# Linear attention with a mixture block on one Trainium2 core: a written-out order of operations in place of planner ranks, and one transfer for w_phi

## The chip, the cores and the metric

The kernel runs on one core of a Trainium2 chip. The metric is the device time of one execution in microseconds, measured on the chip; runs of the same kernel are given with their median, lowest and highest. The inputs are float32 and lie in DRAM, as does the output. The engines are named as in the profile: PE (TensorE, the matrix engine, with PEld for its weight loads), DVE (VectorE), ACT (ScalarE), POOL (GpSimd) and SP (SyncE, which here only issues transfers).

## The reference

Two blocks follow each other. The first is a linear attention with a feature map `phi`, over 8 batches, 8 heads, 576 positions and 64 features per head; the second normalises the rows, applies two dense layers with a ReLU between them and adds the residual.

```
phi(x):  proj = x @ w_phi                      # 64 -> 128 features
         proj = proj - max(abs(proj), axis=-1)
         return concat(exp(proj), exp(-proj))  # 256 features
q_p, k_p = phi(q), phi(k)
kv  = einsum('bhsf,bhsd->bhfd', k_p, v);  z = sum(k_p over s)
out = (q_p @ kv) / (q_p @ z + 1e-6)            # per batch and head
x   = out, heads side by side                  # 8 x 576 x 512
xn  = (x - mean) / sqrt(var + 1e-6) * g_ln
y   = x + relu(xn @ w_ch1) @ w_ch2             # 512 -> 2048 -> 512
```

## The kernel before, in words

**Units.** The attention is done in 32 units, each with two heads. Of the 576 positions 512 are the main part (four chunks of 128 rows per head) and 64 the tail; the tails of the two heads lie side by side in one chunk of 128. A unit loads q, k and v (L676), brings q and k to bfloat16 with the features on the partitions, projects them with w_phi on PE (`pm` for the main part, L984 and L990; `px` for the tails, L943 and L944; `pt` for the transposed projection of q, L999), takes the largest magnitude per row on DVE (L1047 main, L947 tails), takes the exponentials on ACT (L1067, L1111), multiplies v by the scale of k on POOL (L1074 to L1080), sums k against v on PE (L1135, L1141, in `n_bank`), casts the sum (`KV`, L1149 on DVE or L1151 on ACT), multiplies q's features by it (`num`, L1199, L1205), collects and inverts the denominator on DVE (L1221, L1227, L1233) and writes the quotient on POOL as rows of x (L1266, L1270; L1166 moves tails by a transfer). Units 0 to 7 are transposed on PE (L829, L837, copied out of PSUM at L844 on DVE or L846 on ACT); from unit 8 on the inputs are cast (L902 and its neighbours) and transposed by DMA, issued on SP (L921).

**The dense block.** Rows of x are taken in nine groups of 512 tokens. The statistics are taken on DVE (L1338, L1350), the rows are centred and scaled (L1355 on DVE, L1360 on ACT, L1364 on POOL), transposed on PE (L1302) and copied (L1312 on DVE, L1314 on ACT). Then come the first layer (L1431, ReLU at L1439 on DVE or L1441 on ACT) and the second (L1463, with the residual at L1471 to L1480). The last groups go another way (L1597, and L1780 for a product with fewer multiplications). The weights are loaded on POOL's queue: w_ch1 in two pieces at L769, w_ch2 in two at L787.

**What sets the order.** Nothing of the main work is issued where it is written. Each piece is given to the class `Order` (L327) with `add`: the engines that could do it, an estimated time on each, the keys that it reads and writes, the PSUM banks that it takes and gives back, and a rank. `run` then goes through an estimated timeline, event by event: whenever an engine is free there, it takes the ready operation of the lowest rank. The rank is the latest start that the estimates allow, plus an offset from a table, `OFF`, of 32 dictionaries with an entry for each stage. Where several engines could do an operation, the first that is free takes it. The list that comes out is what is issued, engine by engine, and on the chip every engine goes through its own list strictly in order, each instruction waiting for what it needs.

**Fillers.** Up to 75 us of the estimated timeline (`WARM`), whenever PE has nothing ready there, `run` puts a matmul of zeros on PE (`fill`, L2063 and L2064; the first, L2061, stands ahead of it). These matmuls are in the program, so they run whether PE would have had to wait at that place or not.

**The beginning.** Before the planned work DVE clears tiles (L585 to L609), and two casts bring w_phi to the bfloat16 tile `wbk` (L612): rows 0 to 63 for the first head, rows 64 to 127 for the second. The tile `wphi_f` has w_phi twice, one copy per half of the partitions, by two transfers, one on ACT's queue (L564) and one on POOL's (L565). Behind the casts come more clears (`ea`, L616, and `vx`, L596 to L598). These stand in the code as they are issued; the planner only knows that DVE is busy with them.

## Time and profile before

| what | value |
|---|---|
| runs of the kernel | 357.18, 357.02, 356.86 us |
| median | 357.02 us |
| span of the profiled execution | 354.4 us, 9372 instructions |
| profiled execution's own time | the span and what lies around it; the runs' median is 2.6 us above the span |
| PE, DVE, ACT, POOL busy | 98%, 86%, 73%, 53% |
| granted clock of PE | 1.00 in the stretches read |

The profile shows one execution. A group's row has the busy time, the mean duration of one instruction in ns, and the idle time of the engine ahead of such instructions with what ended most of it. A timeline's row has the start in us from the beginning of the span, the time from the first start to the last end, engine, line, operation, tiles and the number of instructions taken together; in brackets stands the idle time ahead and what ended it. A table of stretches has the busy time of each engine between two times. PE's instructions overlap, so a group's mean duration is longer than the distance from one start to the next. Some matmul records are missing from a trace.

### The profile page before, as it was taken

To read this page: it belongs to the slowest core of one execution; us is meant where nothing else is said; L and a number is where in the kernel's file an instruction comes from. 1 tells how busy PE (TensorE), PEld (TensorE's weight loads), DVE (VectorE), ACT (ScalarE), POOL (GpSimd) and SP (SyncE) were. 2 spreads that over 40 slices of the span, in tenths; PEclk is the share of its full clock that TensorE was granted. 3 is DMA by queue.
4 is the path that set the end of the run, shared out by engine and by line. 5 is a ranking of instruction groups with operands and counts; after the bars stand their busy time and mean duration, and the time that the engine had idled before them with its cause. 6 is when DMAs were issued, how large, how long until landed. Compare 5 with 4: busy or idle time off the path is not lost.

```text
span 354.4 us, 9372 instructions
## 1 busy us (share of the span) xinstructions
PE 345.6 (98%) x3606; PEld 221.1 (62%) x3632; DVE 304.8 (86%) x664; ACT 258.5 (73%) x551; POOL 189.3 (53%) x245
## 2 busy tenths in 40 slices
PE   8998999999999999999999999999999999999995
PEld 8987955556554555455545455555555578578884
DVE  5699987899987888988979989897778799999983
ACT  4997988598997996979696975787697833656410
POOL 5499755799644873747478798355546420000000
PEclk9999999999999999999999999999999999999999
DMA  7999999899996888489729242851051005400053
GB/s 210 311 215 287 210 281 246 215 235 258 294 276 175 209 185 215 115 141 280 202 68 209 72 110 47 147 153 35 2 126 63 3 7 116 123 2 3 0 120 118
DMA packets 93676, 53.89 MB, mean 152 GB/s; under 512 B 61104, under 2 KB 88048, under 8 KB 93632
## 3 DMA queue, kind: packets, MB, share of 16 engines
q1 hardware_dynamic: 89392, 47.72, 56.5%
q0 software_dynamic: 3328, 4.49, 7.1%
q10 hardware_dynamic: 912, 1.08, 0.9%
q8 instruction: 28, 0.46, 0.5%
q14 instruction: 16, 0.13, 0.1%
HBM read 36.77 MB, written 9.44 MB: 130 GB/s over the span
## 4 chain that ended last, share of the span: by engine, by line
PE 88%; DVE 8%; ACT 2%; issue 1%; DVEq 0%; ACTq 0%
PE hT_ps L1431 29%; PE ch_ps L1463 22%; PE ch L1597 9%; PE n_bank L2064 4%; PE pm L990 4%; PE n_bank L1141 4%; PE sum L1780 4%; PE num L1199 3%; PE pt L999 2%; DVE m L1047 2%; PE n_bank L1135 1%; DVE numc L1221 1%; PE n_bank L1199 1%; DVE numc L1227 1%; PE n_bank L1205 1%
## 5 line engine op out<-in xcount | busy, mean ns | idle before, releaser
L1431 PE MATMUL hT_ps<-xT,w 128*128 128x512 bf16 x496 | 118.4, 379 | 0.0
L1463 PE MATMUL ch_ps<-w,hT 128*128 128x512 bf16 x362 | 88.9, 379 | 1.3 <-issue 0.3
L1047 DVE TENSOR_REDUCE m<-pm 128x8 f32<-128x1024 f32 x64 | 76.8, 1214 | 7.1 <-PE pm L990 6.5
L1074 POOL TENSOR_TENSOR vv<-v,ek 128x1024 bf16<-128x1024 f32 x32 | 61.1, 1910 | 33.0 <-issue 18.2
L1431 PEld LDWEIGHTS <-w 128*128 128x128 bf16 x496 | 44.2, 98 | 44.0 <-issue 0.8
L1067 ACT ACTIVATE eb<-pm 128x1024 bf16<-128x1024 f32 x64 | 64.5, 1036 | 2.4 <-DVE m L1047 2.3
L1111 ACT ACTIVATE ea<-pt 128x1024 bf16<-128x1024 f32 x64 | 63.8, 1029 | 3.0 <-PE pt L999 2.7
L1266 POOL TENSOR_TENSOR x<-numc,rden 128x128 bf16<-128x128 f32 (+1 forms) x64 | 38.9, 613 | 38.6 <-DVE rden L1233 37.4
L1441 ACT ACTIVATE hT<-hT_ps 128x512 bf16<-128x512 f32 x68 | 40.6, 597 | 24.1 <-PE hT_ps L1431 23.2
L1463 PEld LDWEIGHTS <-hT 128*128 128x128 bf16 x384 | 34.0, 98 | 34.4 <-issue 0.8
L1439 DVE TENSOR_SCALAR hT<-hT_ps 128x512 bf16<-128x512 f32 x56 | 38.5, 687 | 8.6 <-PE hT_ps L1431 8.1
L1199 PEld LDWEIGHTS <-ea 128*128 128x128 bf16 x512 | 24.6, 97 | 10.5 <-issue 1.7
L1141 PE MATMUL n_bank<-vv,eb 128*128 128x65 bf16 x512 | 26.6, 194 | 0.0
L902 POOL TENSOR_TENSOR b<-qk,one 128x1024 bf16<-128x1024 f32 x11 | 20.9, 1896 | 8.9 <-DMA qkT<-b 5.5
L2064 PE MATMUL n_bank<-wz 128*128 128x120 bf16 x347 | 25.0, 224 | 0.1
L1141 PEld LDWEIGHTS <-eb 128*128 128x128 bf16 x512 | 22.3, 98 | 4.3
L1221 DVE TENSOR_TENSOR numc<-num,em 128x390 f32<-128x390 f32 (+1 forms) x40 | 20.3, 513 | 3.3 <-PE num L1199 2.5
L2064 PEld LDWEIGHTS <-wz 128*128 128x128 bf16 x347 | 21.5, 103 | 1.6 <-issue 0.5
L1480 POOL TENSOR_TENSOR o<-o,x 128x512 f32<-128x512 f32 x14 | 16.2, 1154 | 10.5 <-ACT o L1476 10.5
L1338 DVE BATCH_NORM_STATS2 st<-x 128x6 f32<-128x512 bf16 (+1 forms) x40 | 21.3, 569 | 0.4 <-POOL x L1266 0.4
L1199 PE MATMUL num<-KV,ea 128*128 128x65 bf16 x416 | 19.4, 193 | 1.6 <-ACT KV L1151 1.3
L1227 DVE TENSOR_TENSOR numc<-numc,num 128x390 f32<-128x390 f32 (+1 forms) x40 | 20.3, 516 | 0.5
(162 smaller groups left out, 608.7 us busy)
## 6 DMA issues: line engine op xcount, KB each, us to landing
out_dram<-o SPq DMA_DIRECT2D x29, 256.0 KB, 2.6
qk<-in_k_dram SPq DMA_DIRECT2D x12, 512.0 KB, 5.0
qk<-in_q_dram SPq DMA_DIRECT2D x12, 512.0 KB, 6.0
v<-in_v_dram SPq DMA_DIRECT2D x12, 512.0 KB, 4.9
w<-in_moe_w_ch_dram POOLq DMA_DIRECT2D x4, 1024.0 KB, 11.4
qk<-in_k_dram SPq DMA_DIRECT2D x8, 256.0 KB, 6.9
qk<-in_q_dram SPq DMA_DIRECT2D x7, 256.0 KB, 7.5
v<-in_v_dram SPq DMA_DIRECT2D x7, 256.0 KB, 7.4
```

The costliest lines, as they stand in the source:

```text
L1047: nc.vector.reduce_max(out=m, in_=ps, axis=AX.X, apply_absolute_value=True)
L1067: nc.scalar.activation(eb, ps, AF.Exp, scale=(1.0, -1.0)[t])
L1074: eng.tensor_tensor(out=u["vv"][:, :, 0:MX, 0:D], in0=bcast(vb[:, hh, :].rearrange("p (c d) -> p c d", d=D), 1, 2), in1=bcast(e[:, :, 0:MX ...
L1111: nc.scalar.activation(u["EA"][:, t, 0:1024], u["pt"], AF.Exp, scale=(1.0, -1.0)[t])
L1141: nc.tensor.matmul(ps[:, t, c // 4, :], EB[:, t, c, :], vv[:, t, c, :], start=False, stop=(t == 0 and c == MX - 1), skip_group_check=True,)
L1199: nc.tensor.matmul(ps[t][:, i, :], ea(u, t, c), KV[:, t, c // 4, :], start=True, stop=True,)
L1266: eng.tensor_tensor(out=dst, in0=src, in1=by, op=ALU.mult)
L1431: nc.tensor.matmul(st["ps"], w1_sb[:, kc, jj * P : (jj + 1) * P], xT_bufs[g % XB][:, kc::KC, :], start=(kc == 0), stop=(kc == KC - 1),)
L1439: nc.vector.tensor_relu(h_sb, st["ps"])
L1441: nc.scalar.activation(h_sb, st["ps"], AF.Relu)
L1463: nc.tensor.matmul(ch[g, i], hT[g, jj][:, i * P : (i + 1) * P], w2_sb[:, jj, :], start=(jj == 0), stop=(jj == JC - 1),)
L2064: nc.tensor.matmul(warm, wz, wz[:, 0:WN], start=False, stop=False, skip_group_check=True)
```

## The change

**The order.** The table `OFF` and the choice by rank go. In their place stands `ORDER`, which lists for each of POOL, SP, ACT, DVE and PE the numbers of the operations (in the order in which `add` was called) that the engine issues, one after the other. Where an operation could be done by several engines, the list in which it stands decides. `run` still goes through an estimated timeline, but an engine there only takes the next operation of its list, as soon as it is ready; what is left to the estimates is where fillers are put on PE. Many estimates are changed too: a table `LAG` of the time from an end on one engine to a start on another, the time of a matmul, of a change of its tile's height (`INTO`, `OUT`), and of single operations. In `a_trans` the copy of k's transposes now also has the copy of q's among what it depends on, for units whose q is transposed first.

**w_phi.** Both halves of `wphi_f` come by one transfer on ACT's queue, whose source pattern begins with a dimension of two copies and a stride of zero; POOL no longer issues its half. The two casts to `wbk` stand behind the clears of `ea` and `vx`.

```diff
-SLACK = ((0.22, 0.0, 0.0, 1.02), (0.35, 0.6, 1.6, 1.03), (0.22, -1.1, 0.0, 1.28))
+SLACK = ((0.22, 0.0, 0.0, 0.97), (0.35, 0.6, 1.6, 0.97), (0.22, -1.15, 0.0, 1.07))
+LAG = {
+    ("PE", "DVE"): 0.205, ("PE", "ACT"): 0.205, ("PE", "SP"): 0.2, ("PE", "PE"): 0.0,
...
+INTO, OUT = 0.095, 0.108
-OFF = (
-    {
-        "load": 0.0, "trans": -17.5, "trans.copy": -150.8, "mixed": -0.8, "mixed.max": 0.0,
...
+ORDER = {
+    "POOL": """
+        0 7 9 10 22 20 31 86 105 160 128 129 120 142 207 185 194 230 147 193 222 258 277 272 33
...
     def run(self):
-        waiting, free, room, events, done = {}, {}, self.room, [], []
...
+        turn = {engine: [int(n) for n in text.split()] for engine, text in ORDER.items()}
+        for engine, numbers in turn.items():
+            for n in numbers:
+                self.ops[n].engine = engine
...
-                while queue:
-                    item = heapq.heappop(queue)
-                    op = item[2]
...
+                elif place[engine] < len(turn[engine]):
+                    op = self.ops[turn[engine][place[engine]]]
+                    if op.number not in offered or (
+                        op.acquire and room[op.acquire[0]] < op.acquire[1]
+                    ):
                         op = None
+                    else:
+                        place[engine] += 1
...
     wphi_f = consts.tile([P, F], FP32, name="wphi_f")
-    nc.scalar.dma_start(out=wphi_f[0:D, :], in_=w_phi)
-    nc.gpsimd.dma_start(out=wphi_f[D : 2 * D, :], in_=w_phi)
+    nc.scalar.dma_start(
+        out=wphi_f,
+        in_=bass.AP(tensor=w_phi.tensor, offset=w_phi.offset, ap=[[0, 2], [F, D], [1, F]]),
+    )
...
-    for i in range(2):
-        rows = slice(i * D, (i + 1) * D)
-        nc.vector.tensor_copy(out=wbk[rows, i, :], in_=wphi_f[rows, :])
     ea_bufs = []
...
     clear_vx(vx_bufs[1])
+    for i in range(2):
+        rows = slice(i * D, (i + 1) * D)
+        nc.vector.tensor_copy(out=wbk[rows, i, :], in_=wphi_f[rows, :])
...
     def mm(n, cols):
-        return n * (cols / 2.4 + 4.0) / 1000.0
+        return n * (cols / 2.4 + (2.4 if cols > 100 else 3.7)) / 1000.0
...
             add(("DVE", "ACT"), (0.6, 0.93) if n else (0.4, 0.52), rank_cp,
-                lambda e: copy_main(e, cols), r=[("qkT_ps", n)], w=parts,
+                lambda e: copy_main(e, cols),
+                r=[("qkT_ps", n), *([("qkT", j, 1)] if which == (0,) else [])], w=parts,
                 release=None if which == (1,) else (u["res"], 1))
```

The changed kernel's lines have other numbers than those before; in the lists below they are its own, and buffer numbers are one to three lower.

On DVE, at the beginning, this is what stood behind the first clears; `qkT` of the lowest number is unit 0's, and `m` is the tile of the maxima:

```order
L616 MEMSET ea_125 128x2x128
L612 CAST wbk<-wphi_f 64x128 x2
L616 MEMSET ea_127 128x2x128
L596 MEMSET vx_107 128x520
L597 MEMSET vx_107 64x4
L598 MEMSET vx_107 64x4
L1047 TENSOR_REDUCE m_117<-pm 128x8 x2
L844 COPY qkT_141<-qxT_ps 128x128
L947 TENSOR_REDUCE m_117<-px 128x2
L844 COPY qkT_142<-qkT_ps 128x1024
```

And this is what stands there in the changed kernel:

```order
L495 MEMSET ea_122 128x2x128
L495 MEMSET ea_124 128x2x128
L478 MEMSET vx_106 128x520
L500 CAST wbk<-wphi_f 64x128
L479 MEMSET vx_106 64x4
L480 MEMSET vx_106 64x4
L500 CAST wbk<-wphi_f 64x128
L726 COPY qkT_140<-qkT_ps 128x512
L930 TENSOR_REDUCE m_116<-pm 128x8 x2
L726 COPY qkT_141<-qkT_ps 128x1024
L830 TENSOR_REDUCE m_116<-px 128x2
L726 COPY qkT_141<-qxT_ps 128x128
```

The casts have moved behind the clears, one of unit 0's two main copies has come to DVE ahead of the first maxima (before, ACT did both), and the copy of unit 0's tails has left this place.

On PE, around the first projection of unit 8's tails (`qkT` of the lowest number is by then unit 8's; `n_bank` is where the tails' projection goes), before:

```order
L1463 LDWEIGHTS hT
L1463 MATMUL ch_ps<-w_133,hT 128x512
L943 LDWEIGHTS qkT_141
L943 MATMUL n_bank<-wbk,qkT_141 128x256
L944 LDWEIGHTS wbk
L944 MATMUL n_bank<-qkT_141,wbk 128x128
```

And in the changed kernel, where the first two rows are the last of 31 such pairs:

```order
L1947 LDWEIGHTS wz
L1947 MATMUL n_bank<-wz 128x120
L826 LDWEIGHTS qkT_140
L826 MATMUL n_bank<-wbk,qkT_140 128x256
L827 LDWEIGHTS wbk
L827 MATMUL n_bank<-qkT_140,wbk 128x128
```

Sixteen matmuls of the second layer stood ahead of that place before, seven stand there now, and the fillers have come in between. Over the whole program PE has 336 matmuls of zeros where it had 348, of which 305 and 346 stand ahead of the first L1431.

On SP, the loads ahead of the first DMA transpose, of which `qk1_102` is the tile of unit 8 and 9, `qk2_104` that of unit 10 and 11, `b16_2` the bfloat16 copy that is transposed; before:

```order
L676 DMA qx0_88<-in_q_dram 64x4x64 x2
L676 DMA qk1_102<-in_k_dram 128x4x256
L676 DMA qk1_102<-in_q_dram 128x4x256
L676 DMA qk2_104<-in_k_dram 128x4x256
L676 DMA qk2_104<-in_q_dram 128x4x256
L676 DMA vx0_106<-in_v_dram 64x4x64 x2
L676 DMA v1_103<-in_v_dram 128x4x256
L676 DMA v2_105<-in_v_dram 128x4x256
L676 DMA qx1_89<-in_k_dram 64x4x64 x2
L921 DMA_TRANSPOSE qkT0_141<-b16_2_147 128x9x128
```

And in the changed kernel the rows that end with the same load of k and, a few rows further on, the same transpose:

```order
L558 DMA qk1_101<-in_q_dram 128x4x256
L558 DMA qx0_87<-in_q_dram 64x4x64
L558 DMA qx0_87<-in_k_dram 64x4x64
L558 DMA qx0_87<-in_q_dram 64x4x64
L558 DMA qk2_103<-in_k_dram 128x4x256
L558 DMA qk2_103<-in_q_dram 128x4x256
L558 DMA vx0_105<-in_v_dram 64x4x64
L558 DMA qx0_87<-in_k_dram 64x4x64
L558 DMA qk1_101<-in_k_dram 128x4x256
```

k of units 8 and 9 has moved from ahead of q and of the two loads of units 10 and 11 to behind all three. On POOL's queue the two pieces of w_ch2, issued one behind the other before, now stand apart, with the centring of three tiles and two multiplications of v between them; on ACT's queue the first load of v stands behind ACT's first copy of transposes.

More of the change, by code (lines that the diff above doesn't have):

```diff
@@ L393, in run @@
                 if kind == 1:
[L394 to L404 removed]
+                    offered.add(op.number)
@@ L452, in run @@
                     first, last = port[0], port[1]
-                    us = us.us + max(0.0, first - now if now < first else last - now)
-                    if now < last and any(not item[2].engine for item in waiting["POOL"]):
+                    us = us.us + max(0.0, (first if now < first else last) - now - 0.15)
+                    n = place["POOL"]
+                    if now < last and n < len(turn["POOL"]) and turn["POOL"][n] in offered:
                         us += STUCK
```

450 lines of the change are left out of this document (109 added, 341 removed), and 111 rows, old and new, of tables (OFF, ORDER).

## The prediction, made before the changed kernel was run

> **What bounds the kernel now.** The page's first lines come first, then its group of fillers: matmuls of zeros (L2064) that stand on TensorE wherever the planner expected it to wait, and that nobody reads.
>
> ```profile
> span 354.4 us, 9372 instructions
> PE 345.6 (98%) x3606; PEld 221.1 (62%) x3632; DVE 304.8 (86%) x664; ACT 258.5 (73%) x551; POOL 189.3 (53%) x245
> L2064 PE MATMUL n_bank<-wz 128*128 128x120 bf16 x347 | 25.0, 224 | 0.1
> ```
>
> The profiled execution spans 354.4 us and the median of the runs is 357.02, so 2.6 us lie around the span; I carry a change of the span over to the median as it is. A difference of 0.2%, 0.71 us, is about the least that a measurement of this kernel can tell from no change. TensorE is busy for 98%, but 25.0 us of that go by 347 fillers: a full row says nothing until real work is told from zeros.
>
> Next come busy times by stretch: bounds, width, then PE, PEld, DVE, ACT and POOL, granted clock, DMA share and GB/s.
>
> ```profile
> core 0: us, PE busy (x) PEld busy (x) DVE busy (x) ACT busy (x) POOL busy (x), PEclk, DMA share, GB/s
> 0.00:5.00 5.00, 4.01 (x43) 4.01 (x44) 1.53 (x13) 1.74 (x2) 3.85 (x12) 1.00 0.57 166
> 5.00:10.00 5.00, 4.95 (x82) 4.66 (x81) 3.82 (x9) 2.96 (x5) 0.70 (x1) 1.00 1.06 263
> 10.00:15.00 5.00, 4.95 (x79) 4.55 (x78) 3.19 (x6) 4.88 (x16) 2.61 (x3) 1.00 1.11 305
> 15.00:20.00 5.00, 5.00 (x101) 4.88 (x99) 4.78 (x9) 4.93 (x11) 3.30 (x4) 1.00 1.16 305
> 20.00:30.00 10.00, 9.31 (x182) 8.23 (x181) 9.79 (x25) 9.00 (x20) 9.02 (x17) 1.00 1.11 246
> 30.00:40.00 10.00, 8.53 (x172) 7.66 (x169) 10.00 (x27) 8.58 (x23) 7.47 (x11) 1.00 1.16 235
> 40.00:60.00 20.00, 19.89 (x235) 12.67 (x237) 16.11 (x31) 17.27 (x39) 13.36 (x17) 1.00 1.25 265
> 280.00:300.00 20.00, 19.81 (x189) 15.04 (x188) 19.96 (x53) 9.74 (x19) 3.28 (x6) 1.00 0.18 36
> ```
>
> From 40 us on TensorE is dense (19.89 of 20), with real work: of the 348 zero matmuls (the 347 and one of L2061) the program has 346 ahead of the first matmul of the MoE block, and two behind it. The second place where it stands at all is 280 to 300, by 0.19 us, where VectorE is full (19.96). So the time is that first MoE matmul's start plus a dense rest. The start is set by VectorE: 9.79 of 10 and 10.00 of 10 in 20 to 40 us. Only in the first 20 does it have holes: 3.47 in 0 to 5, before data is there, and 15 − 3.82 − 3.19 − 4.78 = 3.21 in 5 to 20.
>
> TensorE's timeline, in rows of start, length, line, tiles and count, fixes the points that I measure from:
>
> ```profile
> 1.07 3.01 PE L2064 MATMUL n_bank<-wz 128*128 128x120 bf16 x28
> 3.87 0.63 PE L829 MATMUL qkT_ps<-ident,qk 128*128 128x128 bf16 x4
> 5.44 0.60 PE L984 MATMUL pm<-wbk,qkT 128*128 128x256 bf16 x4
> ...
> 40.55 1.74 PE L2064 MATMUL n_bank<-wz 128*128 128x120 bf16 x30
> 42.13 0.83 PE L1302 MATMUL xT_ps<-ident,xc 128*128 128x128 bf16 x12
> ...
> 44.42 1.03 PE L1431 MATMUL hT_ps<-xT,w 128*128 128x512 bf16 x4
> ...
> 62.51 1.67 PE L1463 MATMUL ch_ps<-w,hT 128*128 128x512 bf16 x6
> 64.02 0.54 PE L1199 MATMUL num<-KV,ea 128*128 128x65 bf16 x12
> ...
> 66.39 0.27 PE L943 MATMUL n_bank<-wbk,qkT 128*128 128x256 bf16 x1
> ```
>
> The first MoE matmul (L1431) starts at 44.42. A filler costs (42.13 − 40.55) / 30 = 53 ns from start to start; at the very beginning (3.87 − 1.07) / 28 = 100 ns. A matmul of the second layer (L1463) costs (64.02 − 62.51) / 7 = 0.216; the program has seven in that row, and the record of one is missing. The last row is the first projection of unit 8, the first unit whose transposes come by DMA.
>
> **The change: what VectorE has to do before 44.42.** The groups of VectorE's instructions in the first 42.5 us give the prices of what moves, and its timeline the last link.
>
> ```profile
> L844 DVE COPY qkT<-qkT_ps 128x1024 bf16<-128x1024 bf16 x5 | 3.4, 682 | 0.7 <-PE qkT_ps L829 0.7
> L1233 DVE RECIPROCAL rden<-numc 128x3 f32<-128x3 f32 (+1 forms) x10 | 1.5, 174 | 0.0
> L1149 DVE CAST KV<-n_bank 128x260 bf16<-128x260 f32 x3 | 1.2, 415 | 0.1
> L844 DVE COPY qkT<-qxT_ps 128x128 bf16<-128x128 bf16 x5 | 1.1, 213 | 0.5 <-PE qxT_ps L837 0.5
> ...
> 42.55 1.27 DVE L1312 TENSOR_SCALAR xT<-xT_ps,ngln 128x512 bf16<-128x512 bf16 x3
> ```
>
> Ahead of those first xT copies the new list leaves VectorE two reciprocals less (2 × 0.174), one KV cast (0.415) and three tail copies (3 × 0.213), and gives it one half copy of 128x512, for which I take 0.4, a little over half of 0.682. Together −0.35 − 0.42 − 0.64 + 0.4 = **−1.0 us**. What leaves VectorE goes to ScalarE, which has 1.0 and 1.4 us free in 20 to 40, or behind 42.55. Were that cover gone, the 1.0 would be a wait for ScalarE and save nothing.
>
> The new order also puts other instructions into the holes of 5 to 20 us. What that saves lies between 0 and 3.2; no row prices an order that hasn't run, and I take half: **−1.6 us**. There is one independent hint: with the same real work on TensorE ahead of the first L1431, the list is laid out with 304 fillers there (305 zero matmuls with the one of L2061) in place of 345. 41 × 53 ns = 2.2 us less time planned, which lies near 1.0 + 1.6 = 2.6.
>
> **w_phi.** VectorE's casts of it, and the issues at the start, two on ScalarE's timeline and four by the median us to landing:
>
> ```profile
> 3.83 0.22 DVE L612 CAST wbk<-wphi_f 64x128 bf16<-64x128 f32 x1 [1.48 <-DMA wphi_f<-in_w_phi_dram]
> 5.03 0.22 DVE L612 CAST wbk<-wphi_f 64x128 bf16<-64x128 f32 x1 [0.98 <-DMA wphi_f<-in_w_phi_dram]
> ...
> 6.45 2.46 DVE L1047 TENSOR_REDUCE m<-pm 128x8 f32<-128x1024 f32 x2
> ```
>
> ```profile
> 0.74 0.55 ACTq L564 DMA_DIRECT2D wphi_f<-in_w_phi_dram  x1
> 1.33 0.60 ACTq L676 DMA_DIRECT2D qk<-in_q_dram  x1
> ...
> qk<-in_q_dram ACTq DMA_DIRECT2D x1, 256.0 KB, 4.3
> qx<-in_k_dram SPq DMA_DIRECT2D x2, 64.0 KB, 5.8
> wphi_f<-in_w_phi_dram ACTq DMA_DIRECT2D x1, 32.0 KB, 3.1
> wphi_f<-in_w_phi_dram POOLq DMA_DIRECT2D x1, 32.0 KB, 3.7
> ```
>
> VectorE waits 1.48 + 0.98 = 2.5 us for the two halves, and the clears behind the casts (1.2 us, 5.25 to 6.45) come late for it. With the clears ahead, they fall into the wait; VectorE would be ready for the first maxima (L1047) some 1.2 us sooner. Yet those need pm, pm was issued at 5.44, 0.19 after the second cast, and in the new order the transposes of q stand ahead of pm; q lands 4.3 us after an issue at 1.33, at 5.6. So of the 1.2 I count 0.4 as the most that is gained, a third. At worst, the one transfer of 64 KB takes what the 64 KB rows take: issued at 0.74, it lands at 6.5 (0.74 + 5.8), two casts of 0.22 and the 0.19 put pm at 7.2, 1.7 later than 5.44. Those 64 KB loads queue behind 256 KB on their queue and w_phi has nothing ahead of it, so I take **+0.5** between −0.4 and +1.7.
>
> [...]
>
> **The loads and the place of unit 8.** Between the first L1431 and unit 8's first projection stood two fillers, and the new list has 31, right ahead of that projection: +29 × 53 ns = **+1.5 us**, since TensorE is dense there. They are meant to lie over a wait for that unit's transposes; SyncE's timeline shows when those of units 8 to 10 were issued, and the row of issues between 57.0 and 58.5 (unit 8's alone) how long they took to land:
>
> ```profile
> 42.40 0.60 SPq L676 DMA_DIRECT2D qk<-in_k_dram  x1
> 43.05 2.26 SPq L676 DMA_DIRECT2D qk<-in_q_dram  x1
> ...
> 57.13 6.41 SPq L921 DMA_TRANSPOSE qkT<-b  x3
> ```
> ```profile
> qkT<-b SPq DMA_TRANSPOSE x1, 6.4
> ```
>
> Unit 8's lands at 63.5 (57.13 + 6.4) and is needed at 66.39, 22.0 after the first MoE matmul. In the new order nine matmuls of the second layer move from ahead of that place to behind it, and all else ahead of it is the same: 22.0 − 9 × 0.216 + 1.5 = 21.6. I cost the wait at nothing as long as the transposes land by then.
>
> The issues moved past each other on SyncE, ScalarE and GpSimd (v's first half behind a copy on ScalarE, the second half of w_ch2 behind two more multiplications of v) all have an answer of 0: what they feed is needed several us later. The rest of the run has the same matmuls in number and shape and the same end. **Sum:** start 44.42 − 1.0 − 1.6 + 0.5 = 42.3, −2.1; with +1.5 given back −0.6: 354.4 − 0.6 = 353.8 of span, **356.4 us**.
>
> **Rivals.** *Two engines for w_phi* (0.18). [...]
>
> *Unit 8 late* (0.12), slower. Before, k of unit 8 was issued first of its group (42.40); now it stands behind q and the two 512 KB loads of units 10 and 11. Two more of these at 246 to 265 GB/s are 4.1 us. It decides once the transposes land after 42.3 + 21.6 = 63.9, 0.4 past where they were. All of it would cost 3.7; as 57.13 is late for a load issued at 42.40, I let half go into that slack: +1.9, 358.3.
>
> *All holes closed* (0.22): −3.2 in place of −1.6, 354.8; with w_phi at its best 353.9. For it: every engine's list is free to put ready work there. Against: loads ran at 263 to 305 GB/s, so data may not come faster.
>
> *No hole closed* (0.08): 0 in place of −1.6, 358.0. Before TensorE's first transposes now stand 14 fillers, not 28, and it pauses before k lands; the 100 ns fillers show that it is slow there, though the granted clock reads 1.00. [...]
>
> *No effect* (0.10): the list reproduces what the ranks chose as far as the path goes, 357.0.
>
> **How the numbers follow.** The forecast has 0.30, its own range is 355.5 to 357.3. Half of it lies under 356.3 (0.15), 0.11 within the bound, 0.04 above. All holes closed is faster (0.22). Two engines: 0.02, 0.03, 0.13. Unit 8: slower, 0.12. No hole closed: 0.02 same, 0.06 slower. No effect: same, 0.10. Faster 0.39, same 0.26, slower 0.35. Low end 353.9, the best w_phi with all holes closed; high end 358.8, w_phi at +2.9 (356.4 − 0.5 + 2.9).
>
> **What would show it.** The first L1431 near 42.3; VectorE with about 1.6 us of holes in 5 to 20; the casts of w_phi back to back, before 5.5 (right) or behind 5.7 (two engines); pm near 6; TensorE without a pause behind the 31 fillers (a pause there is unit 8 late). It is wrong if the start stays at 44, or if TensorE shows new gaps after 45, where I put none.

## The result, and the profile after

| kernel | runs | median | lowest to highest |
|---|---|---|---|
| before | 4 | 356.94 us | 356.42 to 357.18 |
| after | 4 | 360.64 us | 359.73 to 361.17 |

The ratio of after to before is 1.0106, with a 95% interval of 1.0089 to 1.0123: the changed kernel is slower by 3.2 to 4.4 us. The forecast was 356.4, faster by 0.6. The profiled execution of after took 360.39 us with a span of 358.6, 4.2 above that of before.

The page of after, its first lines and the group of fillers:

```profile
span 358.6 us, 9310 instructions
PE 349.5 (97%) x3620; PEld 221.4 (62%) x3620; DVE 299.8 (84%) x661; ACT 249.0 (69%) x546; POOL 193.0 (54%) x247
L1947 PE MATMUL n_bank<-wz 128*128 128x120 bf16 x335 | 25.4, 231 | 0.0
```

PE is still full on paper. The table of stretches of after, with the columns as before:

```profile
core 0: us, PE busy (x) PEld busy (x) DVE busy (x) ACT busy (x) POOL busy (x), PEclk, DMA share, GB/s
0.00:5.00 5.00, 3.22 (x30) 2.89 (x30) 2.08 (x14) 1.87 (x2) 3.85 (x11) 1.00 0.54 140
5.00:10.00 5.00, 3.04 (x22) 2.42 (x21) 2.17 (x6) 0.12 (x1) 0.18 (x1) 1.00 1.11 213
10.00:15.00 5.00, 5.00 (x70) 4.73 (x68) 1.77 (x2) 3.18 (x5) 0.00 (x0) 1.00 1.11 326
15.00:20.00 5.00, 5.00 (x87) 4.65 (x84) 4.57 (x8) 4.88 (x18) 2.88 (x4) 1.00 1.10 288
...
40.00:60.00 20.00, 19.94 (x227) 12.88 (x227) 15.35 (x33) 16.58 (x42) 11.72 (x14) 1.00 1.12 225
280.00:300.00 20.00, 20.00 (x202) 13.94 (x201) 17.98 (x46) 10.02 (x16) 7.13 (x15) 1.00 0.29 60
```

In 5 to 20 us DVE is busy for 2.17 + 1.77 + 4.57 = 8.51 of 15, so it stands for 6.49, where before it was 3.21. The holes that were to be half filled have doubled. Who ended them is in DVE's waits of that stretch (waiting tile and line, released by, us in total, times, longest):

```profile
DVE qkT L726 <- PE qkT_ps L711: 5.0, 2, 3.0
DVE wbk L500 <- DMA wphi_f<-in_w_phi_dram: 2.1, 1, 2.1
```

5.0 us are waits for transposes on PE, in two pieces. The one of 2.0 us is for q's transposes, which wait for q from DRAM. The one of 3.0 us is for the second unit's: their data had landed by 11.1 (k, issued on SP at 5.16, 5.9 us to landing), but PE came to them only at 13.81, behind 36 fillers. PE's timeline of after:

```profile
1.07 1.61 PE L1947 MATMUL n_bank<-wz 128*128 128x120 bf16 x14
3.46 0.61 PE L711 MATMUL qkT_ps<-ident,qk 128*128 128x128 bf16 x4 [0.78 <-DMA qk<-in_k_dram]
3.86 1.31 PE L1947 MATMUL n_bank<-wz 128*128 128x120 bf16 x11
7.12 0.61 PE L711 MATMUL qkT_ps<-ident,qk 128*128 128x128 bf16 x4 [1.96 <-DMA qk<-in_q_dram]
7.53 1.06 PE L867 MATMUL pm<-wbk,qkT 128*128 128x256 bf16 x4
...
10.03 3.14 PE L1947 MATMUL n_bank<-wz 128*128 128x120 bf16 x36
13.01 0.59 PE L882 MATMUL pt<-qkT,wbk 128*128 128x512 bf16 x2
...
46.23 0.59 PE L1314 MATMUL hT_ps<-xT,w 128*128 128x512 bf16 x2
...
64.27 1.67 PE L1346 MATMUL ch_ps<-w,hT 128*128 128x512 bf16 x7
...
66.15 1.79 PE L1947 MATMUL n_bank<-wz 128*128 128x120 bf16 x31
67.77 0.27 PE L826 MATMUL n_bank<-wbk,qkT 128*128 128x256 bf16 x1
...
124.86 0.40 PE L873 MATMUL pm<-wbk,qkT 64*128 64x128 bf16 x8 [0.59 <-DVE m L930]
```

PE pauses twice, 0.78 us for k and 1.96 for q, and the first `pm` runs at 7.53 in place of 5.44. PE is also slow for longer: four of `pm` take 1.06 (before 0.60), and the 36 fillers (13.01 − 10.03) / 36 = 83 ns each, against 53. The granted clock of 5 to 20 reads 1.00, but that is no reading: the trace's record of the clock begins at 12.30 us in after and at 4.70 in before, both times with 1.00, and the view counts as 1.00 what has no record. The fillers fit a change there: 100 ns each up to 12.30, as at the very start, and 53 behind it make (12.30 − 10.03) / 0.100 + (13.01 − 12.30) / 0.053 = 36. The first MoE matmul (now L1314) starts at 46.23, 1.81 later than before. From there to the second layer's first (64.27) it is 18.04, before 18.09. From there to the end 2.5 more have come in.

Why q is late shows in the issues on ACT's queue in after:

```profile
0.74 1.14 ACTq L444 DMA_DIRECT2D wphi_f<-in_w_phi_dram  x1
1.92 0.42 ACTq L558 DMA_DIRECT2D qk<-in_q_dram  x1
```

The one issue of w_phi takes 1.14 us, where half of it took 0.55, and q behind it is issued at 1.92 in place of 1.33. The median to landing of that load and VectorE's casts of w_phi:

```profile
qk<-in_q_dram ACTq DMA_DIRECT2D x1, 256.0 KB, 5.2
```
```profile
5.25 0.22 DVE L500 CAST wbk<-wphi_f 64x128 bf16<-64x128 f32 x1 [2.08 <-DMA wphi_f<-in_w_phi_dram]
...
5.60 0.22 DVE L500 CAST wbk<-wphi_f 64x128 bf16<-64x128 f32 x1
```

w_phi itself is there by 5.25, before the 5.5 that I gave for the forecast (5.25 to 5.77 in the seven profiles that have after's transfer). q lands at 1.92 + 5.2 = 7.1 instead of 5.6.

Unit 8 in after, on GpSimd and on SyncE:

```profile
58.47 1.89 POOL L785 TENSOR_TENSOR b<-qk,one 128x1024 bf16<-128x1024 f32 x1 [3.98 <-DMA qk<-in_k_dram]
```
```profile
51.73 0.37 SPq L558 DMA_DIRECT2D qk<-in_k_dram  x1
...
60.39 1.53 SPq L804 DMA_TRANSPOSE qkT<-b  x1
```

k of unit 8 is issued at 51.73 (before 42.40), the cast waits 3.98 for it, and the transposes are issued 3.3 later than before. They land 5.6 later, at 66.0, just ahead of the 31 fillers (66.15), so these hide no wait, and PE shows no pause behind them (67.77).

The wait at 124.86 is for maxima that stand on DVE behind three scalings of weights:

```profile
121.04 2.44 DVE L690 TENSOR_SCALAR w<-w,gln 128x512 bf16<-128x512 bf16 x3
...
127.17 0.34 DVE L690 TENSOR_SCALAR w<-w,gln 128x512 bf16<-128x512 bf16 x1
```

### The profile page after: what moved, and what is told of

Same layout as the page of the kernel before. It is cut to its first block, busy times and chain, and to the rows that moved or that the text cites. A ratio compares the mean times of both kernels' runs of the same rounds, so it can differ in the third digit from the quotient of the medians.

```text
span 358.6 us, 9310 instructions
## 1 busy us (share of the span) xinstructions
PE 349.5 (97%) x3620; PEld 221.4 (62%) x3620; DVE 299.8 (84%) x661; ACT 249.0 (69%) x546; POOL 193.0 (54%) x247
## 4 chain that ended last, share of the span: by engine, by line
PE 88%; DVE 5%; ACT 3%; DMA 1%; issue 1%; ACTq 0%; DVEq 0%
PE hT_ps L1314 30%; PE ch_ps L1346 23%; PE ch L1480 10%; PE pm L873 4%; PE n_bank L1024 4%; PE sum L1663 4%; PE num L1082 3%; PE n_bank L1947 3%; PE pt L882 2%; DVE m L930 2%; DMA qk<-in_q_dram 1%; ACT ea L994 1%; PE n_bank L1018 1%; ACT eb L950 1%; PE n_bank L1082 1%; PE n_bank L826 1%
## 5 line engine op out<-in xcount | busy, mean ns | idle before, releaser
L1314 PE MATMUL hT_ps<-xT,w 128*128 128x512 bf16 x496 | 118.6, 379 | 0.0
L1346 PE MATMUL ch_ps<-w,hT 128*128 128x512 bf16 x384 | 89.8, 379 | 0.0
L1314 PEld LDWEIGHTS <-w 128*128 128x128 bf16 x496 | 44.3, 98 | 45.3 <-issue 2.0
L1324 ACT ACTIVATE hT<-hT_ps 128x512 bf16<-128x512 f32 x77 | 45.4, 604 | 29.3 <-PE hT_ps L1314 29.0
L1346 PEld LDWEIGHTS <-hT 128*128 128x128 bf16 x384 | 34.8, 98 | 38.0 <-issue 1.1
L1322 DVE TENSOR_SCALAR hT<-hT_ps 128x512 bf16<-128x512 f32 x47 | 32.0, 686 | 9.4 <-PE hT_ps L1314 9.1
L785 POOL TENSOR_TENSOR b<-qk,one 128x1024 bf16<-128x1024 f32 x15 | 28.3, 1892 | 4.0 <-DMA qk<-in_k_dram 4.0
L1024 PE MATMUL n_bank<-vv,eb 128*128 128x65 bf16 x512 | 24.1, 194 | 0.0
L1024 PEld LDWEIGHTS <-eb 128*128 128x128 bf16 x512 | 21.4, 98 | 2.7
L873 PE MATMUL pm<-wbk,qkT 64*128 64x128 bf16 x448 | 19.9, 217 | 0.6 <-DVE m L930 0.6
L873 PEld LDWEIGHTS <-qkT 64*128 64x128 bf16 x448 | 13.8, 94 | 10.0 <-issue 7.1
```

Of the source, the lines that this page charges most:

```text
L873: nc.tensor.matmul(ps[:, half * 4 + c, :], u["qkT"][rows, cols], wbk[rows, half, :], start=True, stop=True,)
L1024: nc.tensor.matmul(ps[:, t, c // 4, :], EB[:, t, c, :], vv[:, t, c, :], start=False, stop=(t == 0 and c == MX - 1), skip_group_check=True,)
L1314: nc.tensor.matmul(st["ps"], w1_sb[:, kc, jj * P : (jj + 1) * P], xT_bufs[g % XB][:, kc::KC, :], start=(kc == 0), stop=(kc == KC - 1),)
L1324: nc.scalar.activation(h_sb, st["ps"], AF.Relu)
L1346: nc.tensor.matmul(ch[g, i], hT[g, jj][:, i * P : (i + 1) * P], w2_sb[:, jj, :], start=(jj == 0), stop=(jj == JC - 1),)
```

## The experiments

Theory: the single transfer of w_phi holds q back, PE pauses and runs slowly, and the list gains nothing while its data is late; the 31 fillers and the place of unit 8's k cost the rest. The ratios are to the kernel before, run on the same chip. Two rivals went in with the first runs: that w_phi is late because few DMA engines carry it, and that the list itself is slower wherever w_phi comes from.

**w_phi in two transfers, in after.**

```diff
-    nc.scalar.dma_start(
-        out=wphi_f,
-        in_=bass.AP(tensor=w_phi.tensor, offset=w_phi.offset, ap=[[0, 2], [F, D], [1, F]]),
-    )
+    nc.scalar.dma_start(out=wphi_f[0:D, :], in_=w_phi)
+    nc.gpsimd.dma_start(out=wphi_f[D : 2 * D, :], in_=w_phi)
```

> The changed kernel with w_phi in two transfers again (ACT's and POOL's queue); all lists of operations and fillers as in the changed kernel. Theory 'few engines': the one transfer, whose pattern starts with a dimension of 2, is slow itself (landed at about 5.2) and holds back q behind it on ACT's queue (landed at 7.08). Then here q lands near 5.6, the casts are done before 5.4, pm starts near 6.1 instead of 7.53, the first matmul of the dense block comes 1.0 to 1.8 us before 46.23, and the time is 1.0 to 1.8 us below the changed kernel's 360.6. Rival 'the list': the start is late because pm of k stands behind the transposes of q and the loads are in another order; then pm and the first dense matmul move by at most 0.3 us and the time by at most 0.3.

Measured: 359.64 us, ratio 1.0071 (1.0045 to 1.0097). q is issued at 1.34 and its transposes run at 5.92 (7.12 in after); the first MoE matmul starts at 44.43, 1.80 earlier than in after. A start is read from one profile, and profiles with the same beginning differ: 45.69, 46.22 and 46.23 with after's beginning, 43.71 and 44.43 with this one. Of that the ratios give back 0.35%, 1.25 us (their intervals just overlap), and the span 0.4: a new wait takes the rest. PE's row and the two of GpSimd:

```profile
62.98 0.22 PE L1016 MATMUL n_bank<-vv,eb 128*128 128x130 bf16 x1 [1.23 <-DVE m L928]
```
```profile
58.11 1.89 POOL L783 TENSOR_TENSOR b<-qk,one 128x1024 bf16<-128x1024 f32 x1 [5.42 <-DMA qk<-in_k_dram]
...
62.31 0.62 POOL L961 TENSOR_TENSOR vv<-vx,ek 128x260 bf16<-128x260 f32 x1
```

The bracket of PE's row names `m`, but the matmul reads `vv`, whose last piece GpSimd finishes at 62.93, just ahead of it. That piece is behind unit 8's cast, which waits 5.42 us for k. So k's late place does cost, though not where I looked for it.

**w_phi in two transfers, both on ACT's queue.** This keeps the issue time and takes away the pattern with its leading dimension of two.

```diff
-    nc.scalar.dma_start(
-        out=wphi_f,
-        in_=bass.AP(tensor=w_phi.tensor, offset=w_phi.offset, ap=[[0, 2], [F, D], [1, F]]),
-    )
+    nc.scalar.dma_start(out=wphi_f[0:D, :], in_=w_phi)
+    nc.scalar.dma_start(out=wphi_f[D : 2 * D, :], in_=w_phi)
```

> The changed kernel with w_phi in two transfers of 64 rows, both on ACT's queue, one behind the other: the same bytes ahead of q on the same queue and about the same issue time (2 x 0.55 against 1.14 us), but the outermost dimension is 64, not 2. 'Few engines': w_phi lands near 4.2, q near 6.2, pm near 6.7, the time 0.6 to 1.2 us below the changed kernel's. Rival 'issue time': q is late only because ACT issues it 0.6 us later, so q lands near 7.1 as in the changed kernel and the time is within 0.3 us of it. Rival 'the list': no difference either.

Measured: 360.22 us, 1.0097 (1.0078 to 1.0116), within the interval of after. ACT's queue:

```profile
0.75 0.56 ACTq L444 DMA_DIRECT2D wphi_f<-in_w_phi_dram  x1
1.34 0.61 ACTq L445 DMA_DIRECT2D wphi_f<-in_w_phi_dram  x1
1.98 0.61 ACTq L556 DMA_DIRECT2D qk<-in_q_dram  x1
```

VectorE's timeline has the cast of w_phi's second half:

```profile
5.38 0.22 DVE L498 CAST wbk<-wphi_f 64x128 bf16<-64x128 f32 x1 [1.05 <-DMA wphi_f<-in_w_phi_dram]
```

It is no earlier than with one transfer. q is issued at 1.98, lands 5.0 later, at 7.0, and the first MoE matmul starts at 45.53. What stands ahead of q on its queue makes it late, not the pattern with its two copies, and my theory of few engines falls. Whether it is the time of issuing or the 64 KB ahead of q is not told apart here: both are the same in the two kernels.

**The kernel before, with the w_phi part alone.**

```diff
-    nc.scalar.dma_start(out=wphi_f[0:D, :], in_=w_phi)
-    nc.gpsimd.dma_start(out=wphi_f[D : 2 * D, :], in_=w_phi)
+    nc.scalar.dma_start(
+        out=wphi_f,
+        in_=bass.AP(tensor=w_phi.tensor, offset=w_phi.offset, ap=[[0, 2], [F, D], [1, F]]),
+    )
...
-    for i in range(2):
-        rows = slice(i * D, (i + 1) * D)
-        nc.vector.tensor_copy(out=wbk[rows, i, :], in_=wphi_f[rows, :])
     ea_bufs = []
...
     clear_vx(vx_bufs[1])
+    for i in range(2):
+        rows = slice(i * D, (i + 1) * D)
+        nc.vector.tensor_copy(out=wbk[rows, i, :], in_=wphi_f[rows, :])
```

> The kernel before with only the w_phi part of the change (one transfer with the leading dimension of 2, casts behind the clears). 'Few engines': the casts come at 5.2 or later, q lands about 1.4 us later than in the kernel before, the second half of the first transposes is late, and the time is 0.4 to 1.5 us above the kernel before. 'The list': within 0.3 us of the kernel before, or 0.4 below it, since the clears are out of the way.

Measured: 357.79 us, 1.0025 (1.0015 to 1.0035): +0.9 us, and the first MoE matmul at 45.62 in place of 44.42. Without the new list the w_phi part costs a quarter of the loss.

**After without the 31 fillers.**

```diff
-WARM = 75.0
+WARM = 62.0
```

> The changed kernel without the 31 zero matmuls ahead of unit 8's first projection (fillers end at 62 instead of 75 us of the estimated timeline; nothing else differs). Theory 'given back': in the changed kernel the transposes of unit 8 landed at 66.0 and the fillers ran from 66.15 to 67.77, so they hid no wait, and the time falls by 1.4 to 1.7 us. Rival 'a wait takes their place': the transposes, the second half of w_ch2 or DVE's maxima behind it come late anyway, PE waits where the fillers were, and the time is within 0.3 us.

Measured: 359.89 us, 1.0076 (1.0058 to 1.0095): of the 1.6 us that they take, 1.1 come back by the ratios (whose intervals overlap) and 0.75 by the medians. Unit 8's projection follows at 65.68 without a wait. PE stands a few us later instead, ahead of the projection of unit 9's tails:

```profile
71.53 0.27 PE L826 MATMUL n_bank<-wbk,qkT 128*128 128x256 bf16 x1 [0.42 <-ACT ea L843]
```

**k of unit 8 ahead of the other loads**, in the kernel with two transfers; then the same in after, without the fillers and with one transfer.

```diff
-        70 136 246 236 234 238 370 372 242 232 244 140 455 281 240 425 248 451 457 453 429 465
+        70 136 246 244 236 234 238 370 372 242 232 140 455 281 240 425 248 451 457 453 429 465
```

> As the run with w_phi in two transfers, and k of units 8 and 9 issued right behind their q on SP, ahead of the loads of units 10 and 11. In that run the dense block started 1.8 us sooner than in the changed kernel, and PE then lost 1.39 us at 61.4 to 63.0 waiting for v's product on POOL, which stood behind the cast of unit 8, which waited 5.4 us for k. Theory 'k8 late': the wait at 61 goes, and the time falls by 1.0 to 1.4 us against that run's 359.6. Rival: POOL or PE waits for something else there (w_ch2, ScalarE's exponentials), and the time stays within 0.3 us of it.

> The changed kernel (w_phi in one transfer) with k of units 8 and 9 issued earlier on SP and without the 31 zero matmuls. Without the 31 alone, 0.75 us was saved, and PE waited 0.58 us for the transposes of unit 9 instead. 'Given back': with k earlier the transposes come earlier, PE waits nowhere there, and the time is 1.3 to 1.8 us below the changed kernel's 360.6. Rival: the transposes wait for POOL's casts and SP's queue, not for k, and the time is 0.7 us below it as without the 31 alone.

Measured: 358.47 us, 1.0058 (1.0036 to 1.0080) with two transfers: PE's wait at 61 is gone and the profiled span is 2.1 below the first experiment's, of which 0.7 is an earlier start (43.71) that the edit can't have caused; the ratios overlap. In after, without the fillers, it is 360.48 us, 1.0121 (1.0095 to 1.0146): no gain, rather a loss against the run without the fillers alone (1.0076). The earlier k helps at most when the beginning has been mended.

**PE kept busy from the start.** 28 fillers in place of 14 ahead of the first transposes, as before, on top of two transfers and the earlier k (first line of the diff); then also without the 31 (second line).

```diff
-COLD, FIRST = 5.6, 10
+COLD, FIRST = 5.6, 24
...
-WARM = 75.0
+WARM = 62.0
```

> As the run before it here, with 24 zero matmuls written ahead of the planned work in place of 10, so that 28 stand ahead of the first transposes, as in the kernel before. Theory 'slow clock': in the changed kernel PE paused for 0.8 and 2.0 us before 7.1, and pm's four matmuls took 1.06 us where they took 0.60 before, and the 36 zero matmuls ahead of the first pt 3.0 us where 36 warm ones take 1.9. Without the first pause pm takes 0.60, the first pt starts 0.8 to 1.6 us sooner, and so does the dense block: the time falls by 0.8 to 1.5 us. Rival 'loads set the start': pm is quicker but the dense block starts within 0.3 us of the run before it, and so does the time.

> All together: w_phi in two transfers, k of units 8 and 9 earlier, 28 zero matmuls ahead of the first transposes, none of the 31. If the four causes add up, the time is 1.4 to 1.7 us below the run with the warm start, that is near 355.5, and below the kernel before by 1 to 2 us. If a wait takes the place of the 31, within 0.3 us of the run with the warm start.

Measured: 358.84 us, 1.0075 (1.0044 to 1.0106), and 357.83, 1.0036 (1.0012 to 1.0061). The start is now earlier than before, at 42.98 in the first. Yet the first is no faster than the run with k earlier (1.0058): loads of units 8 to 11 land late for it. ACT's cast that waits for one, the PE row behind it and the stretches from 61 us on, all of the first:

```profile
59.65 0.30 ACT L781 CAST b<-qx 128x128 bf16<-128x128 f32 x1 [3.51 <-DMA qx<-in_k_dram]
```
```profile
60.92 0.40 PE L871 MATMUL pm<-wbk,qkT 64*128 64x128 bf16 x8 [2.14 <-ACT ea L992]
```
```profile
61.00:64.00 3.00, 2.21 (x14) 0.86 (x14) 1.23 (x1) 3.00 (x5) 2.07 (x3) 0.80 1.15 152
64.00:68.00 4.00, 3.40 (x44) 2.54 (x44) 0.90 (x3) 2.06 (x5) 4.00 (x6) 0.72 0.60 177
```

A pause of 2.14 us, and behind it the granted clock reads 0.80 and 0.72; in the trace's record that is one spell of half the clock, from 62.83 to 66.24. The profiled execution is the longest of its eight, 362.27 us; the shortest took 357.20.

**w_ch2's two loads earlier.** A theory that falls: that w_ch2, issued later than before, pushes the other loads back. Both loads stand behind operation 147 of GpSimd's list, and the wait for w_ch1 is taken away (`r=[]`).

```diff
-        0 7 9 10 22 20 31 86 105 160 128 129 120 142 207 185 194 230 147 193 222 258 277 272 33
-        231 161 305 299 303 278 293 384 166 369 424 427 415 368 428 363 398 432 403 404 477 496
+        0 7 9 10 22 20 31 86 105 160 128 129 120 142 207 185 194 230 147 161 166 193 222 258 277
+        272 33 231 305 299 303 278 293 384 369 424 427 415 368 428 363 398 432 403 404 477 496
...
-        dma("POOL", V, 1 << 21, emit, r=[("w1 came", 0)],
+        dma("POOL", V, 1 << 21, emit, r=[],
```

> As the run with all three, with both loads of w_ch2 issued right behind the second of w_ch1 on POOL, near 31 us, as in the kernel before; here the estimated timeline puts 92 more zero matmuls on PE, because it expects the weights to hold back other loads. One look only, beside the run in which PE's list is frozen: if the zero matmuls stand where PE waits anyway, it is no slower than that one; if they are on the path, it is slower by up to 92 x 53 ns = 4.9 us.

One run: 362.02 us. But the planner had put 92 more fillers in, so the run says nothing about the loads. From here on the fillers per operation are frozen in a table, with the counts that stand in the kernel compared with: first this kernel again, then after itself with the loads early, then with w_ch1's loads earlier too (their gate from v of units 4 and 5 to units 2 and 3).

```diff
+FILLS = {
+    72: 4, 74: 11, 91: 8, 94: 36, 89: 7, 78: 13, 113: 2, 121: 4, 176: 1,
...
+            for _ in range(FILLS.get(op.number, 0) if op.engine == "PE" else 0):
+                self.filler[3]()
```

> As the run with all three (median 357.8), with both loads of w_ch2 issued right behind the second of w_ch1 on POOL, as in the kernel before; PE's list with all its zero matmuls is kept as it was. In that run and in the one with the warm start the dense block started at 43.0, 1.4 us before 44.4, and PE then waited 2.3, 0.8 and 1.0 us at 58 to 65 for casts of unit 8 on ACT and POOL, which waited for loads that took 8 to 10 us, beside 1 MB of w_ch2 issued at 50. Theory 'loads pushed back': without that megabyte in the way the loads land sooner, the waits at 58 to 65 go for the most part, and the time falls by 1.5 to 3 us, to 355 to 356.3. Rival 'lanes': the loads stand behind SP's own list and its buffers, and the waits stay within 0.5 us.

> The changed kernel with nothing altered but the place of w_ch2's loads (right behind the second of w_ch1); PE's list with all its zero matmuls kept. In the changed kernel PE waited nowhere between 46 and 66 us, so here the theory expects no gain: within 0.5 us of 360.6. If its late loads cost it time by another way (transposes of unit 8 at 66.0 and behind them), up to 1.0 us less.

> As the run with w_ch2 early, and w_ch1 early too: its two loads wait for v of units 2 and 3 in place of 4 and 5, and stand ahead of the first rows of x on POOL, so that the first is issued near 20 (19.26 in the kernel before, 27.98 in the changed one, where DMA's share fell to 0.50 in 25 to 30 us). Theory 'loads pushed back': all waits at 58 to 65 go, and the time is 0 to 1 us below the run with w_ch2 early. Rival: the weights now hold back the first units' own loads, the dense block starts later, and the time is above that run by 0.5 us or more.

Measured: 359.29 us, 1.0089 (1.0054 to 1.0123); 364.93, 1.0222 (1.0197 to 1.0247); 360.33, 1.0084 (1.0061 to 1.0107). None is better than the list without it (1.0036), and the second is clearly worse than after. The dense block starts later, at 45.98 in the first (42.94 without the edit) and at 48.61 in the second (46.23). GpSimd's row and DVE's in the first show a part of the reason:

```profile
31.22 1.78 POOL L677 DMA_DIRECT2D w<-in_moe_w_ch_dram  x2
```
```profile
33.46 0.36 DVE L1112 TENSOR_TENSOR numc<-num,em 128x195 f32<-128x195 f32 x1 [1.15 <-POOL x L1157]
```

Issuing the two loads takes GpSimd 1.78 us; x stands behind them, and DVE waits 1.15 for it, in the stretch where DVE is the bound. The rest of the 3 us I have not followed.

**The maxima of unit 14 ahead of the three scalings** of weights at 121 us, on top of all that was mended so far (ratio 1.0036).

```diff
-        779 861 874 765 766 770 884 879 825 790 905 771 796 894 895 820 900 896 889 914 890 812
+        779 861 874 879 765 766 770 884 825 790 905 771 796 894 895 820 900 896 889 914 890 812
```

> As the run with all three, with DVE's maxima of unit 14 (the second that PE waits for near 124 us, 0.67 us) moved ahead of three scalings of w_ch1 and a cast that took 2.4 us there beside GpSimd's work; PE's list kept. Theory: that wait is part of what the list still loses, and the time falls by 0.5 to 0.8 us against the run with all three. Rival: the scalings are now late for the first layer, and the time is within 0.3 us.

Measured: 356.06 us, 0.9996 (0.9971 to 1.0021); the intervals overlap, but the wait at 124 us is gone. The fall of 1.4 us by the ratios is more than that wait of 0.6, and the executions of both kernels spread over 5 us. The maxima now stand here on DVE, and PE has no gap there:

```profile
120.78 1.21 DVE L938 TENSOR_REDUCE m<-pm 128x8 f32<-128x1024 f32 x1
```

**PE's pauses by themselves.** In after both are filled (28 fillers first, and 50 in place of 11 ahead of q's transposes, by the first diff); in before one is made (18 fillers in place of 28 ahead of k's, by the second).

```diff
-COLD, FIRST = 5.6, 10
+COLD, FIRST = 5.6, 24
...
-    72: 4, 74: 11, 91: 8, 94: 36, 89: 7, 78: 13, 113: 2, 121: 4, 176: 1,
+    72: 4, 74: 50, 91: 8, 94: 36, 89: 7, 78: 13, 113: 2, 121: 4, 176: 1,
```
```diff
-COLD, FIRST = 5.6, 10
+COLD, FIRST = 5.6, 0
```

> The changed kernel with its pauses of PE in the first 7 us filled with zero matmuls (14 more ahead of the first transposes, 39 more ahead of those of q); all else kept, w_phi in one transfer. Theory 'slow clock': pm's four matmuls take 0.60 in place of 1.06 us, the 36 zero matmuls ahead of the first pt 1.9 in place of 3.0, the first dense matmul starts 0.8 to 1.8 us sooner, the time falls by 0.6 to 1.8 us. Rival 'loads set the start': it starts within 0.4 us of where it did, and so ends.

> The kernel before with the ten zero matmuls ahead of the planned work left out, so that PE pauses for about 1 us ahead of the first transposes, as in the changed kernel; nothing else differs. Theory 'slow clock': matmuls up to about 8 us take twice the time (pm 1.06 in place of 0.60), and the dense block starts 0.5 to 1.5 us later, the time is 0.4 to 1.5 us above the kernel before. Rival: the clock's rise does not depend on a pause that short, pm takes 0.60 and the time is within 0.2 us.

Measured in after: 360.33 us, 1.0087 (1.0074 to 1.0100). The same 36 fillers in that run:

```profile
9.12 2.05 PE L1957 MATMUL n_bank<-wz 128*128 128x120 bf16 x36
11.02 0.59 PE L892 MATMUL pt<-qkT,wbk 128*128 128x512 bf16 x2
```

They take (11.02 − 9.12) / 36 = 53 ns each again, with the same late q, the clock's record begins at 5.73 in place of 12.30, and the start comes at 45.30, 0.9 earlier; the time falls by 0.3 (medians) to 0.7 us (ratios), less than the intervals can tell. In before, the pause of 0.78 us makes the first `pm` take 0.92, moves the start from 44.42 to 45.24 and costs 0.28%: 357.62 us, 1.0028 (1.0015 to 1.0042). So a pause in place of ten fillers costs by itself. That slow matmuls are how is likely, but this profile alone does not show it: in the run with the tails earlier, below, the first `pm` takes 1.06 with 28 fillers and no pause.

**Two tries on what is left around 60 us**, on top of the mended list: the casts of tails behind what they wait for, and the last load of tails of units 8 to 11 earlier on SP's list.

```diff
-        231 161 305 299 303 278 293 384 166 369 424 427 415 368 428 363 398 432 403 404 477 496
+        231 161 305 299 303 278 293 384 166 369 424 415 427 368 428 363 398 432 403 404 477 496
...
-        340 316 412 407 413 330 423 410 386 414 334 431 438 439 482 344 437 484 474 475 471 476
+        340 316 412 407 413 330 410 386 414 334 423 431 438 439 482 344 437 484 474 475 471 476
```
```diff
-        70 136 246 244 236 234 238 370 372 242 232 140 455 281 240 425 248 451 457 453 429 465
+        70 136 246 244 236 234 238 232 370 372 242 140 455 281 240 425 248 451 457 453 429 465
```

> As the run before it here, with the casts of the tails of units 8 and 9 moved behind ScalarE's exponentials of unit 7 and behind GpSimd's product for unit 7; in the profile of the warm start ACT stood 3.5 us and POOL 6.2 us at these casts, for tails that landed at 59.6, and PE waited 2.3, 0.8 and 1.1 us for what stood behind them. Theory 'a late load blocks a list in order': these waits shrink, executions spread less, and the time falls by 1 to 2 us to 355 to 356.3. Rival: the transposes of units 8 and 9 come later by as much, PE waits at 65 to 72 instead, and the time is within 0.4 us.

> As the run with the maxima ahead, with the last of the four tail loads of units 8 to 11 moved ahead of the two 512 KB loads of units 10 and 11 on SP, so that ScalarE's and GpSimd's casts of those tails don't wait for it; PE's list kept. Theory 'a late load blocks lists in order': in bad executions PE waited up to 4 us near 58 to 65 us behind these casts; that goes, the executions spread less (upper ones under 358), and the median falls by 0.4 to 1.2 us, to 355 to 355.7, below the kernel before by 1 to 2 us. Rival: the tails wait for bandwidth, not for their place, or the two large loads are late in turn: median and spread as before, within 0.4 us.

Measured: 358.37 us, 1.0031 (1.0007 to 1.0054): no gain, the wait has only moved, to unit 8's transposes:

```profile
64.35 0.28 PE L834 MATMUL n_bank<-wbk,qkT 128*128 128x256 bf16 x1 [1.29 <-DMA qkT<-b]
```

And 356.52, 1.0012 (0.9985 to 1.0039), no different from the list without it. Its executions lie between 354.86 and 359.63, those of before on the same chip between 356.09 and 357.53.

**The single transfer put back into that last kernel**, all else equal.

```diff
-    nc.scalar.dma_start(out=wphi_f[0:D, :], in_=w_phi)
-    nc.gpsimd.dma_start(out=wphi_f[D : 2 * D, :], in_=w_phi)
+    nc.scalar.dma_start(
+        out=wphi_f,
+        in_=bass.AP(tensor=w_phi.tensor, offset=w_phi.offset, ap=[[0, 2], [F, D], [1, F]]),
+    )
```

> As the run with the tails earlier, with w_phi in one transfer again. It prices the transfer in a list where nothing later hides it: the issue of 1.14 in place of 0.55 us ahead of q makes q land 1.2 us later and PE, with its 28 zero matmuls ahead, pauses for it. Theory: the first dense matmul starts 1.0 to 1.8 us later, and the time is 0.8 to 1.8 us above that run. Rival: lists and loads later on swallow the delay, and the time is within 0.4 us.

Measured: 358.00 us, 1.0043 (1.0026 to 1.0060): +0.31%, 1.1 us, by the ratios (whose intervals overlap) and 1.5 by the medians. The start of the MoE block and the stretch of 8 to 12.5 us with two transfers, and then the same with one:

```profile
42.94 3.62 PE L1322 MATMUL hT_ps<-xT,w 128*128 128x512 bf16 x16
```
```profile
8.00:12.50 4.50, 4.50 (x77) 4.21 (x75) 2.50 (x5) 4.12 (x6) 0.00 (x0) 1.00 1.05 297
```
```profile
45.70 1.67 PE L1324 MATMUL hT_ps<-xT,w 128*128 128x512 bf16 x7
```
```profile
8.00:12.50 4.50, 4.50 (x52) 4.24 (x50) 2.74 (x3) 1.94 (x2) 0.00 (x0) 0.62 1.12 301
```

The start moves by 2.76 us. Behind PE's pause of 2.10 us for q the granted clock is 0.62 and PE gets through 52 matmuls in place of 77. The record has the full clock from 4.89, half of it from 8.30 to 11.71, and the full one again.

## Why the prediction was wrong

**The work moved off DVE, −1.0: right.** The rows of before and of after up to DVE's first copy of xT (at 42.55 and 44.47):

```profile
0.00:42.55 42.55, 39.19 (x689) 36.43 (x694) 35.58 (x91) 34.63 (x78) 29.50 (x47) 1.00 1.07 248
```
```profile
0.00:44.47 44.47, 40.03 (x654) 35.91 (x655) 34.63 (x87) 33.62 (x77) 28.25 (x45) 1.00 0.95 214
```

DVE does 35.58 − 34.63 = 0.95 us less.

**The holes half filled, −1.6: this step failed, and with it the sign.** DVE's idle time ahead of that copy went from 42.55 − 35.58 = 6.97 to 44.47 − 34.63 = 9.84, +2.87. I treated the holes as room that an order could fill. They were waits (5.0 of the 6.49 in 5 to 20 us, by the waits): 2.0 for q, and 3.0 for PE, which went through 36 fillers at 83 ns each (53 under the full clock) while the second unit's data lay ready from 11.1 on. Before, too, DVE's waits in that stretch were for w_phi (1.0) and for results of PE (2.7). The growth goes when q is on time and PE is kept busy: DVE's idle time ahead of its first copy is 9.8 in after, 8.0 with w_phi in two transfers, 7.3 with k of unit 8 earlier as well, and 6.3 to 6.6 in the five kernels that have 28 fillers ahead besides (those that start at 42.94 to 43.07). So with its data on time and PE kept busy the list saves 0.4 to 0.7 of the 1.6, and not in 5 to 20 us, where 3.9 to 4.1 us of holes are left, but in the first 5. The argument that data may not come faster stood in my own text, against *All holes closed*. The hint of 41 fillers less was none: that count comes out of the planner's estimates, which the change altered too and which know nothing of q's later arrival.

**w_phi, +0.5: the mechanism was left out and the size is two to three times as large.** I priced when w_phi lands and kept q at 5.6, though my own rows had q issued behind it on ACT's queue (0.74 and 1.33) and I wrote that `pm` now stands behind q's transposes. The issue takes 1.14 us instead of 0.55, q lands at 7.1, and PE pauses and is slow afterwards. Measured as time: +0.9 us in the old list, +1.1 (medians 1.5) in the mended one, 1.25 in after, all within the range for this term, up to +1.7. Measured as the start, which is what the sum added it to, one profile each: +1.2, +2.8 and +1.8, of which two lie above that range. No run shows the +2.9 of the high end: the start moved by at most 2.8 and the time by at most 1.25 (medians 1.5), with w_phi there by 5.25 to 5.77.

**The first MoE matmul at 42.3: it started at 46.23.** The two steps above are the difference: −0.95 + 2.87 is 1.9 for DVE's copies, 1.81 for PE. The list with its data on time and PE kept busy does start early, at 42.94 to 43.07, 1.4 to 1.5 ahead of before; the change as made never got there.

**The fillers, +1.5: right as time on PE** (67.77 − 66.15 = 1.6), but taking them out gave back only 1.1 us by the ratios, 0.75 by the medians; a wait ahead of unit 9's tails comes up in their place.

**Unit 8, 0: right in after, by luck.** Its transposes were issued 3.3 us later than before and landed at 66.0, and PE came to the fillers ahead of their place at 66.15 only because the whole block had moved back by 1.8. With the start mended the late k cost 1.2 us on PE, by a path that I had not followed: GpSimd goes through its list in order, and `vv` of another unit is queued behind the cast that waits for k.

**The rest dense, 0: wrong.** From 64.27 to the end 2.5 us were added: 29 fillers (1.55), a wait of 0.59 at 124.86 for the maxima behind three scalings, and one at 328.42, of which PE's row gives 0.30:

```profile
328.42 0.39 PE L1663 MATMUL sum<-ea,v 128*128 128x256 bf16 x2 [0.30 <-DVE v L1589]
```

The 0.19 us of PE's idle time in 280 to 300 are gone; some 0.2 I can't assign. I had taken the same matmuls for the same time, though the list moves DVE's work in the rest as well; the wait at 328 was not tried.

**The rivals.** *Two engines for w_phi* was not shown: no run tells how many engines carry the transfer. The run with both transfers on ACT's queue speaks against the pattern of two copies as the cause: without it the second half was there at 5.38, where both were by 5.25 in after, and the time is 1.0097 against 1.0106. The packets don't tell the two kernels apart either: with the one transfer 128 packets of 512 B, 27 ns each, start between 2.84 and 4.53, which is 128 × 27 ns / 1.69 us = 2.0 at a time; those of the two plain transfers on the same queue start between 2.88 and 4.66, 1.9 at a time, and the trace does not name a packet's engine. In before, one transfer in place of two, on two queues, cost 0.9 us, with the casts moved as well. *Unit 8 late* was real, but the late start hid it. *No hole closed* (358.0) was nearest in sign and mechanism, and with its second half, PE pausing ahead of k and slow there (0.78 us, and fillers of 100 ns), nearer than I gave it credit for; no case had the holes growing.

**What stays open.** The mended lists are level with before (0.9996 and 1.0012, both intervals across 1), so no version beats both kernels. Their fastest executions are 1.1 to 1.2 us below the fastest of before, their slowest 2 us above its slowest. Waits around 60 us for loads of units 8 to 11 show in the profiles of the longest executions; why those loads are late in some executions alone is not settled. Nor is why q's load itself takes 5.0 to 6.0 us when it is issued at 1.9 and 3.6 to 4.7 when it is issued at 1.3: only 0.6 of its lateness is the later issue, and whether the rest is the 64 KB ahead of it on its queue was not tried.

## What to carry to other kernels

A transfer's price includes what it holds up on its queue (w_phi's issue took 1.14 us in place of 0.55, and q behind it landed at 7.1 in place of 5.6): ask first what stands behind it, and whether that is what the kernel's first work waits for. An idle stretch can be filled by a new order only if something is ready there (here 5.0 of 6.49 us were waits for PE); read who ended the wait before counting on it. When an engine with a strict list waits, follow what is queued behind the waiting instruction (`vv`, behind a cast that waited 5.42 us), and look for the price there.
